# Memory-augmented attention in segments: turning the softmax rows by VectorE block transposes instead of TensorE

## The chip, the cores and the metric

The kernel runs on one core of a Trainium2 chip. A core has a matrix engine (TensorE, PE in the profile; PEld is its weight load), a vector engine (VectorE, DVE), a scalar engine (ScalarE, ACT), GpSimd (POOL) and a queue engine that issues transfers (SyncE, SP). SBUF is the working memory of 128 partitions; PSUM takes what TensorE writes. The metric is the time of one execution on the device in microseconds.

## The reference: what is computed

The input is x of 2048 rows by 512. Four layers follow each other, each added to its input after a layer normalization: attention A, dense B, attention A, dense B, with the same weights in both rounds.

```python
def _A_ref(x, mem0, Wq, Wk, Wv, Wo, seg_len):      # seg_len 32, 32 heads of 128, memory of 8 rows
    for s in range(n_seg):                         # 64 segments
        h = concatenate([mem, xs])                 # 40 rows
        q, k, v = h @ Wq, h @ Wk, h @ Wv           # per head
        scores = where(mask, q @ k.T * scale, -1e9)
        p = softmax(scores)
        o = (p @ v) @ Wo
        mem = o[:, :M, :]
        outs.append(o[:, M:, :])
def _B_ref(x, w1, w2):                             # 512 -> 1376 -> 512
    return relu(x @ w1) @ w2
x = x + A(layernorm(x)); x = x + B(layernorm(x)); x = x + A(layernorm(x)); x = x + B(layernorm(x))
```

The memory rows that a segment puts out are the memory of the next one, so the 64 segments of a round follow each other.

## The kernel before

The two rounds run together. In step k the kernel handles segment k of the first round and segment k - 2 of the second (`DELTA`), 66 steps in all, 62 of them with both. The 40 rows of both segments stand side by side as 80 columns of `HT`, so that one weight load serves both.

A step has these parts. `queries_keys` multiplies `HT` with the weights of four heads at a time (16 matmuls of 80 columns for queries, 16 for keys) and evicts the result to `qT` and `kT`. `step_values` computes the values (`values`, L1040). The 32 heads are handled in five units (`UNITS`, L18): three of eight heads, and the last eight heads in two units of four. For each unit `scores` (L1116) multiplies queries and keys into PSUM tile `sp` (L1133), adds the mask into `es` (`block`, L1144), subtracts the row maximum (`top`, `sub`), takes the exponential on ScalarE (`exp`, L1155), sums and inverts (`total`, `recip`) and multiplies into the bf16 tile `P` (`mul`, L1175, on VectorE or GpSimd). Then the rows have to be turned, since the next matmul wants keys on the partitions: `turn` (L1181) multiplies blocks of `P` of 128 columns by an identity on TensorE into another PSUM tile `tp`, and two `keep` evictions (L1194), one for each half of the partitions, copy it to `PT`, each multiplied by a column of ones and zeros (`half`) so that the other half becomes zero. `attend` (L1205) multiplies the values with `PT` (L1217) and evicts to `OT`; `project` (L1233) multiplies by `Wo` into the PSUM tile `st`, accumulating over all heads. From there the memory columns go to the `HT` of the next step (`ev`, with which that step can start), and the rows to `OX`.

`finish` (L899) handles the dense layer of a step: `OX` is turned by a transfer (`turn`, on the SP queue) into `y`, added to the residual `xg` (64 rows of 512: 32 of each round), normalized (`layernorm`, L744: `stats`, `aggr`, the power -0.5 on GpSimd in `rstd`, `norm`), turned on TensorE (`turned`, L764, four matmuls), and multiplied by `w1` and `w2` (`dense_layer`, L785). `total` adds the result in two instructions, each of 64 rows by 256. The first round's 32 rows are normalized and turned again for the second attention; `carry`, `widen` and `narrow` copy rows on GpSimd, and `store` writes the output.

The order of all instructions is made by a planner in the kernel's own text, before the program is built (`Plan`, L289). Each operation has a list of engines with a cost for each (`t_act`, `t_dve`, `t_pool`, `t_copy`), and what it reads and writes. TensorE's operations stand in an order fixed by a table of places (`PLACE`: a place within a step for each operation and phase); those of the other engines are taken by priority, worked out backwards from their users, among those that can start within `LOOK` of the earliest. Each operation that may run on either of two engines goes to the one on which it would end first. Matmuls can run as whole tiles of 128 columns of weights or as two tiles of 64 (`PAIRED` names those that take the halves); a switch between the forms is charged. The planner also charges for TensorE's instructions being fetched in blocks of 256 (`BLOCK`, `FETCH`). Transfers are issued on the SP queue in the planner's order: value loads, the turning of `OX`, stores.

Of the kernel before, what the change touches and what calls it, by code (L numbers as in the profile page):

```python
# [8 lines left out]
BF = mybir.dt.bfloat16  # L9
# [21 lines left out]
LOOK = 0.0763052  # L31
PERIOD = 26.155362
PLACE = {
# [1342 lines left out]
```

## Time and profile before

| What | Value |
|---|---|
| three timed runs | 1589.28, 1590.21, 1590.93 us (median 1590.21) |
| profiled execution: span from the first to the last instruction | 1588.6 us (no other time of it is given) |
| busy in the span: PE | 1569.5 us, 99%, 45458 matmuls |
| ACT | 1165.2 us, 73%, 3073 instructions |
| DVE | 1082.3 us, 68%, 2957 instructions |
| POOL | 314.3 us, 20%, 667 instructions |
| granted TensorE clock, mean | 0.998 |

The profiled execution is another one than the timed runs; its span stands 1.6 us below their median. Busy time is the union of an engine's instructions, which overlap by their pipelines, above all on PE; what an instruction costs in a stream without gaps is read from the distance between the starts of two. In the timeline each line has the start, the time from the first start to the last end of a group, engine, line of the kernel, operation, what it writes and reads, and the number of instructions; in brackets stands the idle time of the engine before it and what ended it. In the groups the numbers after the bar are busy time, mean duration in ns of one, and the engine's idle time before them.

### The profile page before, as it was taken

The numbers are of one execution on the slowest core, as the hardware profiler recorded it, in microseconds if no ns is written. First come the engines' busy times: TensorE is split into PE (matmuls) and PEld (weight loads), VectorE is DVE, ScalarE is ACT, GpSimd is POOL, SyncE is SP. The second block draws the span as 40 slices with busy tenths as digits, with TensorE's granted clock in tenths as the row PEclk, the third lists the DMA queues.
The fourth block names the chain that finished last, engine by engine and source line by source line (L and its number), as shares of the span: only waits on it lengthen the run. The fifth ranks groups of instructions, "written<-read, shape, count | busy, mean of one in ns | idle before, by whom it ended". The sixth has DMA issues, their size and how long they took to land.

```text
span 1588.6 us, 100346 instructions
## 1 busy us (share of the span) xinstructions
PE 1569.5 (99%) x45458; PEld 1411.1 (89%) x45458; DVE 1082.3 (68%) x2957; ACT 1165.2 (73%) x3073; POOL 314.3 (20%) x667
## 2 busy tenths in 40 slices
PE   8999999999999999999999999999999999999998
PEld 5689999999999989999989999999998998898887
DVE  4566766766776776686676677677667667667665
ACT  4667777777777777777777777777777777777774
POOL 5112112212112212121121221211211121112110
PEclk9999999999999999999999999999999999999999
DMA  9711111111111111111111111111111111111100
GB/s 371 243 44 30 26 33 32 29 35 37 25 39 31 35 29 33 29 32 40 26 36 27 35 26 42 37 26 38 25 35 28 33 33 29 33 25 22 28 21 9
DMA packets 76540, 70.89 MB, mean 45 GB/s; under 512 B 50920, under 2 KB 62416, under 8 KB 76112
## 3 DMA queue, kind: packets, MB, share of 16 engines
q1 hardware_dynamic: 70096, 44.14, 13.1%
q0 software_dynamic: 4992, 19.40, 3.4%
q8 instruction: 356, 5.83, 1.6%
q10 hardware_dynamic: 1024, 0.93, 0.2%
q14 instruction: 72, 0.59, 0.1%
HBM read 31.53 MB, written 9.96 MB: 26 GB/s over the span
## 4 chain that ended last, share of the span: by engine, by line
PE 97%; DMA 1%; DVE 1%; POOL 1%; ACT 0%; issue 0%; DVEq 0%; POOLq 0%
PE work L726 40%; PE st L726 19%; PE fill L1048 16%; PE fill L726 8%; PE fill L821 5%; PE work L1217 5%; PE work L1133 4%; DMA xg<-in_A_x_dram 0%; DMA y<-OX 0%; DMA w_sb<-in_B_w_dram 0%; ACT HT L982 0%; POOL Wo_sb L537 0%; PE fill L711 0%; DVE ln L749 0%; POOL ln L736 0%
## 5 line engine op out<-in xcount | busy, mean ns | idle before, releaser
L726 PE MATMUL work<-HT,Wq_sb 128*128 128x80 bf16 (+2 forms) x10400 | 361.8, 201 | 3.1 <-ACT HT L982 3.1
L726 PE MATMUL work<-HT,Wk_sb 128*128 128x80 bf16 (+2 forms) x10416 | 362.7, 201 | 0.8 <-ACT HT L982 0.8
L726 PEld LDWEIGHTS <-Wq_sb 128*128 128x128 bf16 (+1 forms) x10400 | 330.9, 104 | 20.8 <-issue 6.0
L726 PE MATMUL st<-OT,Wo_sb 128*128 128x80 bf16 (+1 forms) x8448 | 345.5, 201 | 0.0
L726 PEld LDWEIGHTS <-Wk_sb 128*128 128x128 bf16 (+1 forms) x10416 | 327.1, 104 | 17.3 <-issue 2.0
L726 PEld LDWEIGHTS <-Wo_sb 128*128 128x128 bf16 x8448 | 315.7, 100 | 13.0 <-issue 12.7
L1048 PE MATMUL fill<-Wv_sb,HT 128*64 128x512 bf16 x2112 | 273.6, 381 | 1.1 <-DVE HT L984 1.0
L982 ACT CAST kT<-work 128x320 bf16<-128x320 f32 (+1 forms) x523 | 218.3, 418 | 68.6 <-PE work L726 31.1
L982 ACT CAST qT<-work 128x320 bf16<-128x320 f32 (+1 forms) x516 | 215.7, 418 | 67.5 <-PE work L726 47.2
L1198 ACT ACTIVATE PT<-work,half 128x160 bf16<-128x160 f32 (+1 forms) x515 | 231.3, 463 | 20.1 <-PE work L726 12.7
L982 ACT CAST OT<-work 128x320 bf16<-128x320 f32 (+1 forms) x461 | 186.2, 420 | 50.7 <-PE work L1217 50.6
L982 ACT CAST vw<-fill 128x512 bf16<-128x512 f32 x229 | 134.1, 586 | 113.3 <-PE fill L1048 109.8
L1144 DVE TENSOR_TENSOR es<-work,maskb 128x320 f32<-128x320 f32 (+2 forms) x330 | 136.2, 413 | 99.7 <-PE work L1133 93.2
L924 DVE TENSOR_TENSOR xg<-xg,y 64x512 f32<-64x512 f32 x65 | 44.2, 680 | 227.2 <-DMA y<-OX 226.6
L731 POOL TENSOR_SCALAR ln<-ln 32x1 f32<-32x1 f32 (+2 forms) x159 | 46.6, 293 | 566.7 <-DVE ln L752 561.0
L1155 ACT ACTIVATE es<-es 128x320 f32<-128x320 f32 (+2 forms) x330 | 136.1, 413 | 24.4 <-DVE es L1151 16.2
L1048 PEld LDWEIGHTS <-HT 128*64 128x64 bf16 x2112 | 98.9, 110 | 57.0 <-DVE HT L984 1.2
L1151 DVE TENSOR_TENSOR es<-es,mx 128x320 f32<-128x320 f32 (+2 forms) x330 | 136.3, 413 | 4.9
L1148 DVE TENSOR_REDUCE mx<-es 128x8 f32<-128x320 f32 (+2 forms) x330 | 133.9, 406 | 5.4
L1158 DVE TENSOR_REDUCE sm<-es 128x8 f32<-128x320 f32 (+2 forms) x330 | 133.4, 404 | 5.1 <-ACT es L1155 2.2
L1175 DVE TENSOR_TENSOR P<-es,sm 128x320 bf16<-128x320 f32 (+1 forms) x269 | 126.9, 472 | 3.3
L1133 PEld LDWEIGHTS <-qT 128*40 128x40 bf16 x4096 | 93.3, 97 | 35.6 <-ACT qT L982 13.6
(96 smaller groups left out, 2164.8 us busy)
## 6 DMA issues: line engine op xcount, KB each, us to landing
V<-vw SPq DMA_DIRECT2D x248, 48.0 KB
V<-vh SPq DMA_DIRECT2D x120, 64.0 KB
Wq_sb<-in_A_Wq_dram POOLq DMA_DIRECT2D x2, 2048.0 KB, 23.2
Wk_sb<-in_A_Wk_dram POOLq DMA_DIRECT2D x2, 2048.0 KB, 28.6
Wo_sb<-in_A_Wo_dram POOLq DMA_DIRECT2D x2, 2048.0 KB, 39.4
vh<-vg SPq DMA_DIRECT2D x32, 128.0 KB
xb<-in_A_x_dram SPq DMA_DIRECT2D x16, 128.0 KB
Wv_sb<-in_A_Wv_dram POOLq DMA_DIRECT2D x1, 2048.0 KB, 13.2
```

What stands on the lines that cost most here:

```text
L726: nc.tensor.matmul(out_[u:v, :], lhsT=lhsT[:, u:v], rhs=rhs, start=start, stop=stop, tile_position=(0, u), **more)
L821: nc.tensor.matmul(yp[64 * u:64 * u + 64, 0:256], lhsT=hT[:, fc, :], rhs=w2_sb[:, fc, 256 * u:256 * u + 256], start=(fc == 0), stop=(fc == ...
L982: nc.scalar.copy(out=out_, in_=in_)
L1048: nc.tensor.matmul(vp[64 * b:64 * b + 64, :], lhsT=cols(c4), rhs=Wv_sb[:, c4, n * 512:(n + 1) * 512], start=(c4 == 0), stop=(c4 == NC4 - 1 ...
L1133: nc.tensor.matmul(v[64 * g2:64 * g2 + L, a, i, b, :], lhsT=qT[:, hi, a * L:(a + 1) * L], rhs=kT[:, hi, a * L:(a + 1) * L], start=True, st ...
L1144: nc.vector.tensor_tensor(out=flat(es[:, A]), in0=flat(sp[:, A]), op=ALU.add, in1=maskb[:, a_lo:a_hi, :].unsqueeze(2).to_broadcast([128, n ...
L1148: nc.vector.tensor_reduce(out=mx[:, As], in_=es3(), axis=AX.X, op=ALU.max)
L1151: nc.vector.tensor_tensor(out=es3(), in0=es3(), op=ALU.subtract, in1=mx[:, As].unsqueeze(2).to_broadcast([128, ns * na, L]))
L1155: nc.scalar.activation(out=es[:, A], in_=es[:, A], func=ACTF.Exp, scale=SCALE)
L1158: nc.vector.tensor_reduce(out=sm[:, As], in_=es3(), axis=AX.X, op=ALU.add)
L1175: (nc.gpsimd if eng == POOL else nc.vector).tensor_tensor(out=o, in0=flat(es[:, A]), op=ALU.mult, in1=sm[:, As].rearrange("p (a s) -> p a ...
L1198: nc.scalar.activation(out=o, in_=i, func=ACTF.Copy, scale=half[:, b:b + 1])
```

## The change

1. `BLOCKED = (0, 1, 2, 3)`: in all units the softmax rows are turned without TensorE. The scores of two heads are laid down next to each other, so that in `es` and `P` the two heads alternate from key to key. A pair of bf16 values then makes one 4-byte element. `mul` (VectorE only, two instructions for a unit of eight heads) writes `P`; `turn` is one `nc.vector.transpose` of 4-byte elements, which turns blocks of 32 by 32 in place and puts them into `es`. Narrow copies place the blocks in `PT`: for each half of the partitions `stay` copies the blocks that lie in the right partitions (64 partitions), `shift` the others in two instructions (32 partitions each, 8 and 32 keys for each pair of heads). They run on ScalarE or GpSimd. The rest of `PT` is zero from three fills at the start, so `half` is not used for it. `attend` reads its moving operand at every second bf16 element (`spread`), since the heads alternate. The PSUM tile `tp` is gone; `es` has three buffers instead of two.
2. The residual rows stand as 128 partitions by 256 columns instead of 64 by 512 (the second half of the columns in other partitions). So the instructions of `finish` on VectorE take half the elements: `layernorm_halves` computes statistics of half rows, exchanges them between the partition halves (`swap`, two tiny copies) and combines them. `turned` needs two matmuls instead of four, `total` one instruction instead of two; the turning transfer of `OX` has two blocks instead of four; `carry` and `widen` are two instructions each, and the store is two transfers.
3. The order is planned anew: other `PLACE`, `PAIRED` and `AHEAD` tables, and `LOOK` of 0.1008 instead of 0.0763. In the program that results, 12,000 query and key matmuls run as half-width ones instead of 7,840, TensorE has 46,090 matmuls instead of 45,458, and 289 switches of the tile form instead of 299. GpSimd makes no product of the softmax any more.

```diff
-LOOK = 0.0763052
+LOOK = 0.1007903
+BLOCKED = (0, 1, 2, 3)
+def t_place(n):
+    return 0.21 + 1.16e-3 * n
...
-    p_es = ring("es", 2, [128, 8 * L], F32)
-    p_PT = ring("PT", 3, [128, 2, 4, 2, L])
+    p_es = ring("es", 3, [128, 8 * L], F32)
+    p_PT, p_PM = ring("PT", 3, [128, 4, 2, 128]), ring("PM", 0, [128, 2, 4, 2, L])
...
+        parts += [([t], 0.6, ["PT0"]) for t in p_PT.tiles]
...
+    def layernorm_halves(x, keys, quick=False):
+        def stats():
+            nc.vector.bn_stats(out=ln[:, 0:6], in_=x[:, :])
+        def swap(eng):
+            for u in range(2):
+                copy_on(eng, ln[64 * u:64 * u + 64, 8:14], ln[64 - 64 * u:128 - 64 * u, 0:6])
+        def aggr():
+            nc.vector.bn_aggr(out=ln[:, 6:8], in_=ln[:, :].rearrange("p (s f) -> p s f", s=2)[:, :, 0:6])
+        def norm():
+            nc.vector.tensor_scalar(out=xn[:, 0:256], in0=x[:, :], scalar1=ln[:, 6:7], scalar2=ln[:, 7:8],
+                                    op0=ALU.subtract, op1=ALU.mult)
+        plan.op(DVE, t_dve(256), stats, r=keys, w=[ln])
+        plan.op((ACT, DVE), (0.2, 0.2), swap, w=[ln])
...
-    def turned(xn, n, columns, copies):
+    def turned(xn, n, columns, copies, blocks=NC4):
...
-            for c4 in range(NC4):
-                across(cols, tp[:, c4 * n:(c4 + 1) * n], xn[:, c4 * 128:(c4 + 1) * 128], columns)
+            for c4 in range(blocks):
+                across(cols, tp[:, c4 * wide:(c4 + 1) * wide], xn[:, c4 * 128:(c4 + 1) * 128], columns)
...
-            for u in range(2):
-                cs = slice(256 * u, 256 * u + 256)
-                nc.vector.tensor_tensor(out=to[RB, cs], in0=x[RB, cs], in1=yp[64 * u:64 * u + 64, 0:256], op=ALU.add)
+            nc.vector.tensor_tensor(out=to[:, :], in0=x[:, :], in1=yp[:, 0:256], op=ALU.add)
...
+            for u in range(2):
+                def store(u=u):
...
+                plan.op(SP, 0.78, store, r=[ob], lag=2.45)
...
+    def moved(eng, out_, in_):
+        if eng == ACT:
+            nc.scalar.copy(out=out_, in_=in_)
+        else:
+            nc.gpsimd.tensor_copy(out=out_, in_=in_)
...
-        plan.op(PE, nx * na * 0.0358, turn, r=[*[("P", p, b, x) for b in range(2) for x in xs], "ident"], w=[tp, PT],
-                tile=EITHER, count=nx * na)
-
+        def turn():
+            nc.vector.transpose(out=es[:, 0:64 * nj].rearrange("p (j k) -> p j k", k=64),
+                                in_=P[:, 0:512].bitcast(F32).rearrange("p (j k) -> p j k", k=64)[:, mine, :])
...
+        plan.op(DVE, 0.09 + 1.06e-3 * 64 * nj, turn, r=[*where, "PT0"], w=[es, PT])
         for b in range(2):
-            def keep(eng, b=b):
...
-            copy_op(n, keep, r=[tp, PT, "half"], w=[(PT, b)], more=MASKED)
+            def stay(eng, b=b):
+                i, o = turned_pairs()
+                R = slice(64 * b, 64 * b + 64)
+                moved(eng, o[R, :, b, 0:L], i[R, :, 0:L])
+            def shift(eng, b=b):
+                i, o = turned_pairs()
+                for c, w in ((0, L - 32), (1, 32)):
+                    R, T = slice(64 * b + 32 * c, 64 * b + 32 * c + 32), slice(64 * b + 32 - 32 * c, 64 * b + 64 - 32 * c)
+                    moved(eng, o[R, :, b, 32 - 32 * c:32 - 32 * c + w], i[T, :, 32 * c:32 * c + w])
...
+        def spread(a, i, g):
+            if p in BLOCKED:
+                return PT[:, (a - a_lo) * nx + i, :, :].rearrange("p b (q g) -> p b q g", g=2)[:, :, 0:L, g]
...
-                                             rhs=PT[:, a, 2 * i + h2, :, :], start=True, stop=True, tile_position=(0, u))
+                                             rhs=spread(a, i, h2), start=True, stop=True, tile_position=(0, u))
```

More of the change, by code (lines that the diff above doesn't have):

```diff
@@ new lines @@
+    ("*layernorm.aggr", 1): -200649.813, ("*layernorm.norm", 1): 22.495, ("*layernorm.stats", 1): 17.877,
+    ("*make_mask", 1): -30.313, ("*prepare_more.zero_w2", 1): -0.818, ("*rstd.power", 1): -162.931,
+    ("*rstd.raise_", 1): -0.19, ("*turned.keep", 1): 4.73, ("*turned.turn", 1): 79044.517,
+    ("*values.ev", 1): 63605.211, ("*zero_columns.zero", 1): -130570.662, ("attend.ev", 0): 57.345,
+    ("attend.ev", 1): -2.014, ("attend.ev", 2): -18232.828, ("attend.mm", 0): 121954.026, ("attend.mm", 1): 2.485,
@@ new lines @@
+    ("prep_x.cp", 1): -6.04, ("prepare.first_exp", 1): -2.682, ("prepare.get_memory", 1): -123728.422,
+    ("prepare.keep", 1): 2763.322, ("prepare.place", 1): 31317.055, ("prepare.turn", 1): -3.242,
+    ("prepare.zero", 1): 93635.535, ("prepare.zero_bank", 1): -0.856, ("prepare.zero_none", 1): 32782.739,
+    ("project.ev", 0): -10.294, ("project.ev", 1): -5.822, ("project.ev", 2): -0.574,
+    ("project.first", 1): -76604.132, ("project.mm", 0): -7842.728, ("project.mm", 2): 136193.946,
+    ("project.rows", 0): -0.268, ("project.rows", 1): -3.828, ("project.rows", 2): -80261.41,
@@ new lines @@
+    ("scores.turn", 0): 1.73, ("scores.turn", 1): -0.078, ("turned.keep", 0): -0.114, ("turned.keep.da", 0): 9.527,
+    ("turned.keep.da", 1): 52.509, ("turned.keep.da", 2): 200547.065, ("turned.keep.db", 0): 14.324,
+    ("turned.turn", 0): -106636.935, ("turned.turn.da", 0): -1.821, ("turned.turn.da", 1): -20239.724,
+    ("turned.turn.da", 2): 0.245, ("turned.turn.db", 0): -36.958, ("values.ev", 0): 148933.802,
+    ("values.mm", 0): -0.137, ("values.mm", 1): -1.627, ("values.mm", 2): 6.543, ("zero_columns.zero", 1): 0.082,
@@ L741, in rstd @@
         else:
-            plan.op(POOL, 0.80, power, r=["half"], w=[ln])
+            plan.op(POOL, 0.95, power, r=["half"], w=[ln])
     def layernorm(x, keys, R=slice(0, 128), quick=False):
@@ L787, in dense_layer @@
         n = 2 * SEG
-        xnT, xn = p_xm.buf(), layernorm(x, keys, slice(0, n), last)
-        turned(xn, n, ident[:, 0:n], [(NC4 * n, lambda: xnT[:, :, :], same, [], [xnT])])
+        xnT, xn = p_xm.buf(), layernorm_halves(x, keys, last)
+        turned(xn, n, ident[:, :], [(NC4 * n, lambda: xnT[:, :, :], same, [], [xnT])], 2)
         hT = p_h.buf()
@@ L902, in finish @@
         last = k == nsteps - 1
-        x, keys = xg[k % 2], [("x", k % 2, a) for a in range(2)]
+        x, keys = x_of[k % 2], [("x", k % 2, a) for a in range(2)]
         if 0 in act:
@@ new lines, in scores, with mul, turn, keep @@
+        if not blocked:
+            def mul(eng):
+                o = P[:, :].rearrange("p (a c) -> p a c", a=2)[:, a_lo:a_hi, 128 * xs[0]:128 * xs[-1] + 128]
+                o = o.rearrange("p a (s k) -> p a s k", k=64)[:, :, :, 0:L]
+                (nc.gpsimd if eng == POOL else nc.vector).tensor_tensor(
+                    out=o, in0=es[:, A].rearrange("p (a s k) -> p a s k", s=ns, k=L), op=ALU.mult,
+                    in1=sm[:, As].rearrange("p (a s) -> p a s", a=na).unsqueeze(3).to_broadcast([128, na, ns, L]))
+            plan.op((POOL, DVE), (t_pool(n), t_dve(n)), mul, r=[es, sm], w=where)
+            tp = b_work.buf()
+            def turn(cols):
+                rhs = ident[:, :].rearrange("p (g q) -> p g q", g=2)[:, :, 0:L]
+                for a in range(a_lo, a_hi):
+                    for i, x in enumerate(xs):
+                        z = nx * a + i
+                        c0 = 256 * a + 128 * x
+                        across(cols, tp[:, z * 2 * L:(z + 1) * 2 * L], P[:, c0:c0 + 128], rhs)
+            PT = p_PM.buf()
+            plan.op(PE, nj * 0.0358, turn, r=[*where, "ident"], w=[tp, PT], tile=EITHER, count=nj)
+            for b in range(2):
+                def keep(eng, b=b):
+                    o = PT[:, a_lo:a_hi, 0:2 * nx, b, :]
+                    i = tp[:, A].rearrange("p (a g q) -> p a g q", g=2 * nx, q=L)
+                    if eng == ACT:
+                        nc.scalar.activation(out=o, in_=i, func=ACTF.Copy, scale=half[:, b:b + 1])
+                    else:
+                        nc.vector.tensor_scalar_mul(out=o, in0=i, scalar1=half[:, b:b + 1])
+                copy_op(n, keep, r=[tp, PT, "half"], w=[(PT, b)], more=MASKED)
+            return PT
```

274 lines of the change are left out of this document (143 added, 131 removed), and 226 rows, old and new, of tables (PAIRED, PLACE).

## The prediction

> **What bounds the kernel now.** I read the page's busy shares and chain first, then the stages, the waits of TensorE and the timeline of a step. Views: the page, with instruction fetches among the DMA queues; the stages, whose columns are busy time and instruction count of PE, PEld, DVE, ACT and POOL, granted clock, DMA share, GB/s; and the waits of PE.
>
> ```profile
> span 1588.6 us, 100346 instructions
> ...
> PE 1569.5 (99%) x45458; PEld 1411.1 (89%) x45458; DVE 1082.3 (68%) x2957; ACT 1165.2 (73%) x3073; POOL 314.3 (20%) x667
> ...
> q8 instruction: 356, 5.83, 1.6%
> ...
> PE 97%; DMA 1%; DVE 1%; POOL 1%; ACT 0%; issue 0%; DVEq 0%; POOLq 0%
> ```
> ```profile
> 520.00:720.00 200.00, 200.00 (x5887) 183.17 (x5884) 140.21 (x378) 151.99 (x402) 41.25 (x87) 1.00 0.14 32
> 1478.27:1481.57 3.30, 3.30 (x134) 2.75 (x131) 3.27 (x10) 2.62 (x6) 0.00 (x0) 1.00 0.15 35
> ```
> ```profile
> PE work L726 <- ACT HT L982: 4.0, 14, 0.3
> ```
>
> In a steady stretch TensorE is busy for 200.00 of 200 us at full clock. Its longest wait in total is 4.0 us, at the memory columns that open a step. Every other engine has room (DVE 70%, ACT 76%, POOL 21% of the stretch). So a nanosecond taken from the TensorE stream is a nanosecond of the span, as long as no new wait appears. A busy PE is not PE at its peak, so its prices are read from start to start in the timeline:
>
> ```profile
> 781.90 0.26 PE L1133 MATMUL work<-kT,qT 128*40 128x40 bf16 x8
> ...
> 782.45 0.31 PE L726 MATMUL work<-ident,P 128*64 128x80 bf16 x8
> 782.59 0.21 PE L1217 MATMUL work<-PT,V 128*64 128x80 bf16 x2
> ...
> 783.30 1.32 PE L726 MATMUL st<-OT,Wo_sb 128*128 128x80 bf16 x32
> 784.46 0.24 PE L726 MATMUL work<-ident,P 128*128 128x80 bf16 x2
> ...
> 787.32 0.20 PE L1217 MATMUL work<-PT,V 128*128 128x80 bf16 x1
> ...
> 788.04 0.26 PE L726 MATMUL fill<-ident,xr 128*128 128x32 bf16 x4
> 788.15 0.73 PE L726 MATMUL st<-OT,Wo_sb 128*128 128x80 bf16 x16
> ```
> ```profile
> 803.58 0.52 PE L726 MATMUL fill<-xnM,w_sb 128*128 128x64 bf16 x12
> 803.93 0.74 PE L726 MATMUL work<-HT,Wq_sb 128*128 128x80 bf16 x16
> 804.60 0.28 PE L1133 MATMUL work<-kT,qT 128*40 128x40 bf16 x8
> ```
> ```profile
> 1478.27 0.74 PE L726 MATMUL work<-HT,Wq_sb 128*64 128x80 bf16 x32
> 1478.84 0.74 PE L726 MATMUL work<-HT,Wk_sb 128*64 128x80 bf16 x32
> ```
>
> A whole 80-column matmul costs (784.46 - 783.30) / 32, about 36 ns. A pair of half-width ones costs 0.14 / 4 = 35 ns in the turn and 0.57 / 16 = 36 ns in queries and keys: the same. A 64-column one costs 0.35 / 12 = 29 ns. The group ahead of 804.60 takes 0.67 for 16 x 36 = 0.575, so a switch between whole and half-width tiles costs 0.097.
>
> **The change part by part.** TensorE first: the turns that go, and the attend matmuls that stay.
>
> ```profile
> L1217 PE MATMUL work<-PT,V 128*128 128x80 bf16 x516 | 61.1, 202 | 1.1 <-DVE PT L1200 1.1
> L1217 PE MATMUL work<-PT,vw 128*128 128x80 bf16 x508 | 60.8, 202 | 0.0
> L726 PE MATMUL work<-ident,P 128*128 128x80 bf16 x756 | 59.3, 202 | 0.2 <-DVE P L1175 0.2
> L1217 PE MATMUL work<-PT,vw 128*64 128x80 bf16 x1032 | 54.1, 202 | 0.5 <-ACT vw L982 0.5
> L1217 PE MATMUL work<-PT,V 128*64 128x80 bf16 x1016 | 53.3, 202 | 0.0
> ...
> L726 PE MATMUL work<-ident,P 128*64 128x80 bf16 x536 | 22.0, 201 | 0.4 <-DVE OT L984 0.4
> ```
>
> 1. Softmax turns (`scores.turn`): 756 whole and 536 / 2 = 268 pairs, 1024 x 0.0357 = 36.5 us off the stream.
> 2. Turns of normalized rows (`turned`): after the dense layer four 32-column matmuls (0.11, from 788.04 to 788.15) become two of 64 columns (0.058), 64 times: 3.3 us off. Ahead of the dense layer four of 64 columns (0.117) become two of 128, twice the columns, so nothing to speak of.
> 3. Order: tile switches fall from 299 to 289 by the two listings of the programs, 10 x 0.097 = 1.0 off. Some 4,200 more half-width query and key matmuls stand in the new order, at the same price per pair: 0.
>
> The stream loses 36.5 + 3.3 + 1.0 = 40.8 us, or 0.64 us of a 23.4 us step. Now what could be put on it.
>
> 4. Instruction supply. The page's fetch queue brought 356 packets of 16 KB, one for every 256 of PE's instructions. Turns at 36 ns per instruction pair go, and half-width groups (64 instructions in 0.575 us) crowd together: in the new order one stretch per step holds 8 + 32 + 3 x 64 instructions in about 2.0 us, next to values at 16 in 0.87. Spaced by the prices above, the quickest tenth of the blocks of 256 falls to 2.9 to 3.06 us (34 blocks). The row of 1478.27 shows 134 + 131 instructions in 3.30 us with no idle: 256 in 3.2. So a turnaround above 3.2 us is excluded. At 3.2 the blocks would wait 9.5 us in all (the shortfall summed over them), at 2.9 nothing; I take the middle, 5. [...]
>
> 5. Query and key evictions. What a hand-over costs shows at the step's opening, where nothing covers it:
>
> ```profile
> 1468.97 0.73 PE L726 MATMUL st<-OT,Wo_sb 128*128 128x80 bf16 x16
> ...
> 1470.01 0.66 PE L726 MATMUL work<-HT,Wq_sb 128*128 128x80 bf16 x14 [0.30 <-ACT HT L982]
> ```
> ```profile
> 1469.74 0.21 ACT L982 CAST HT<-st 128x64 bf16<-128x64 f32 x1 [0.32 <-PE st L726]
> ```
>
> The stream of 16 ends at 1468.97 + 0.575 = 1469.545, ScalarE starts 0.195 later, takes 0.21, and PE goes on 0.06 after that: 0.465 us. A 320-element eviction (0.43) makes it 0.68. In the new order the shortest distance from a unit's last key group to its scores is 4 half-width turns and one group, 0.11 + 0.57 = 0.68: no margin, where it was 0.87. Covered it costs 0; if ScalarE is busy with a short instruction when it should start (0.2 late, 62 steps), 12. Nearest is the covered case; I take 2. The opening itself has as many uncovered steps in both orders: 0.
>
> 6. The softmax chain. For the last unit, on DVE and ACT:
>
> ```profile
> 785.37 0.49 DVE L1175 TENSOR_TENSOR P<-es,sm 128x160 bf16<-128x160 f32 x1
> ```
> ```profile
> 786.24 0.68 ACT L1198 ACTIVATE PT<-work,half 128x160 bf16<-128x160 f32 x2 [0.18 <-PE work L726]
> ```
>
> Scores end at 782.00, the product at 785.86, the masked evictions at 786.92, and attend starts at 787.32: 0.34 of its 5.3 us are left (0.06 goes to the hand-over). In the new chain the product is followed by a block transpose of 128 elements and six narrow copies, all on ScalarE for this unit. Durations are bounded by these rows:
>
> ```profile
> L1198 ACT ACTIVATE PT<-work,half 128x320 bf16<-128x320 f32 x251 | 133.1, 533 | 0.0
> ...
> L1198 ACT ACTIVATE PT<-work,half 128x160 bf16<-128x160 f32 x263 | 97.8, 396 | 19.7 <-PE work L726 12.3
> ...
> L1144 DVE TENSOR_TENSOR es<-work,maskb 128x160 f32<-128x160 f32 x136 | 43.7, 321 | 27.6 <-PE work L1133 21.3
> ...
> L957 POOL COPY xg<-vx 32x512 f32<-32x512 f32 x64 | 39.0, 609 | 12.0 <-DVE vx L940 8.3
> ...
> L1175 DVE TENSOR_TENSOR P<-es,sm 128x160 bf16<-128x160 f32 x75 | 34.2, 455 | 0.2
> ...
> L811 DVE TENSOR_SCALAR hT<-fill 128x256 bf16<-128x256 f32 x63 | 26.8, 425 | 0.5 <-PE fill L726 0.3
> ...
> L998 POOL COPY HT<-xnA 128x128 bf16<-128x128 bf16 x63 | 18.4, 292 | 477.2 <-PE work L726 453.4 <-PE fill L1048 23.7
> ...
> L982 ACT CAST HT<-st 128x64 bf16<-128x64 f32 x62 | 13.2, 213 | 21.2 <-PE st L726 21.2
> ...
> L982 ACT CAST kT<-work 128x160 bf16<-128x160 f32 x31 | 8.9, 291 | 3.7 <-PE work L726 2.2 <-ACT vx L982 0.3
> ```
>
> A transpose has no row. As one pass over 256 elements it takes 0.425 (0.32 for 160), as two passes twice that; I take one pass, the nearest operation being a 4-byte copy. Six copies at 0.213 end to end are 1.28, less with the overlap that back-to-back rows show (two of 0.396 in 0.68). So the new chain ends 0.32 + 1.1 + 0.2 = 1.6 us after the product, 0.5 later than the 1.06 now, and the new order gives this unit 5.7 to 6.2 us instead of 5.3: covered, by 0.2 to 0.6. Cost 0. The cover is the dense matmuls and projections that stand between; without it each 0.1 us would cost 62 x 0.1 = 6 us.
>
> 7. Off the path. By the listings ACT drops 133.1 + 97.8 = 231 us of masked evictions and gets 1317 narrow copies at 0.213 to 0.291 (280 to 383), some 130 other evictions at 0.4 and 168 tiny copies of statistics: +140 to +240 on 1165, at most 90% of the new span. GpSimd gets 645 placing copies at about 0.29, +190 on 314, and loses a product per step. DVE gets 330 transposes (at most 140 us) and 247 more product pieces (0.321 to 0.455 each, 79 to 112), and loses 145 masking evictions and half the elements of each dense-path instruction (512 wide becomes 256): about even. SP issues a second store per step and transposes half as much; the store's issue is queued ahead of the value loads, which have most of a step. At the start three zeroings of the new tiles delay the first normalization: 0 to 2 us, taken as 1.
>
> **Sum.** The profile names no time for this execution but its span, 1588.6; the timed runs lie 1.6 above it at the median (1589.28, 1590.21, 1590.93). So 1588.6 - 40.8 + 5 + 2 + 1 = 1555.8, plus 1.6: 1557.
>
> **The rivals.**
> (a) Instructions come at the slow end (step 4): 9.5 in place of 5, with a late eviction or two: 1563.
> (b) The softmax chain is late. DVE's product of 160 elements takes 455 ns where the addition of the same size takes 321; in the timeline GpSimd's copy of the carried rows runs beside the slow ones. With 645 more GpSimd copies, subtraction and product of each unit may pay 0.134 each; a two-pass transpose adds 0.3. That is 0.3 us beyond the cover per step, 62 x 0.3 = 19: 1576. Against it stands that the other three units have 7 to 10 us. [...] This needs 0.66 us per step to eat the whole gain.
> (c) Slower: the attend matmuls. Their moving operand, two adjacent 40-column blocks until now, is read at every second element (`spread`), which no row of this trace does. It costs nothing if the stream keeps its pace; at half pace 1024 whole and 1024 pairs of them pay 36 ns more, 73 us: 1557 + 73 = 1630. It decides from 20 ns each on. [...]
> (d) The change does not relieve TensorE: excluded as far as rows go, since the turns stand in a stream without idle time.
>
> **How the numbers follow.** Forecast 0.60 (1547 to 1562), (a) 0.12, (b) 0.19, (c) 0.09. Low end: steps 4 to 7 cost nothing, 1590.2 - 40.8 = 1549, and 2 less for how far run and sum may stand apart: 1547. High end: (b) with step 4 at its limit, 1576 + 5, 1581; beyond it lie (c) and the worst of (b), together under 0.2. Within 0.2% (3 us, about what can be told from no change) needs (b) or (c) at exactly the gain: 0.02. Slower: (c) 0.09 and 0.02 of (b). Faster: 0.87.
>
> **What would show it.** A steady stretch with PE still at 200 of 200 us and a step of 22.8 us in place of 23.4; no `ident,P` matmuls; attend rows still at 36 ns from start to start (72 would be (c)); fetch packets still one per 256 instructions, with gaps in PE that no engine explains if (a) holds; waits of attend or of the first projection on ACT, POOL or DVE if (b) holds, and the transpose's mean against 0.425. The prediction is wrong if attend slows, if the chain of the last unit exceeds 5.7 us, or if PE's stretch is not full.

## The result

The changed kernel takes 1679.91 us (median of four runs, 1679.63 to 1680.78); the kernel before took 1590.41 beside it (1589.28 to 1590.93). The ratio is 1.0568, with a 95% interval of 1.0553 to 1.0583. It is slower by 5.7%, where 1557 us and a range of 1547 to 1581 were predicted.

First the page of the changed kernel (line numbers are now its own: L1030 is the placing copy on ScalarE, L1032 the one on GpSimd, L1024 and L1026 the evictions on ScalarE and VectorE, L1185 scores, L1286 the block transpose, L1327 attend, L737 the shared matmul line).

```profile
span 1679.1 us, 103987 instructions
...
PE 1596.4 (95%) x46090; PEld 1399.8 (83%) x46090; DVE 1031.5 (61%) x3287; ACT 1374.8 (82%) x4173; POOL 499.9 (30%) x1403
...
q8 instruction: 361, 5.91, 1.5%
...
ACT 43%; PE 42%; DVE 9%; issue 5%; DMA 1%; POOL 1%; SPq 0%; DVEq 0%; ACTq 0%; POOLq 0%
```

The last line is the chain of work that ended last. It was 97% PE; now ScalarE holds 43% of it. The stage and the waits of PE, as read before:

```profile
520.00:720.00 200.00, 194.58 (x5750) 172.41 (x5748) 127.62 (x399) 168.22 (x504) 62.06 (x174) 1.00 0.12 28
```
```profile
PE work L1327 <- ACT PT L1030: 21.8, 59, 1.2
PE work L1185 <- ACT qT L1024: 12.6, 46, 0.9
...
PE work L1185 <- ACT kT L1024: 3.3, 4, 2.2
```

TensorE is no longer busy for 200 of 200 us but for 194.58, at the same clock, and ScalarE went from 152 to 168. A step takes 24.79 us in place of 23.50 (mean distance of the memory-column evictions over the middle steps). Attend waits for the placing copies and the scores wait for the queries' eviction. The named waits are the smaller part: a busy PE is not PE at its peak, and the time from start to start of its matmuls, beyond what the prices of the prediction give, is some 130 us more than before (the 90 us lost and the 40 us of matmuls that went). Most of the excess lies just ahead of attend, between attend and the next projection, and ahead of the scores, all of them places that need something from ScalarE.

So the timeline of ScalarE at the end of one step, in which the last two units are placed, with VectorE's product and transpose of the last unit and the attend that follows:

```profile
828.73 0.34 ACT L1221 ACTIVATE es<-es 128x160 f32<-128x160 f32 x1 [0.26 <-DVE es L1286]
828.97 2.01 ACT L1030 COPY PT<-es 64x80 f32<-64x80 f32 x8
831.01 0.40 ACT L1024 COPY ln<-ln 64x6 f32<-64x6 f32 x2
831.44 0.75 ACT L1024 CAST OT<-work 128x320 bf16<-128x320 f32 x2
832.08 1.49 ACT L1030 COPY PT<-es 64x80 f32<-64x80 f32 x6
833.59 0.80 ACT L1024 CAST OT<-work 128x320 bf16<-128x320 f32 x2
```
```profile
830.12 0.32 DVE L1279 TENSOR_TENSOR P<-es,sm 128x160 bf16<-128x160 f32 x1
...
830.48 0.31 DVE L1286 STREAM_TRANSPOSE es<-P 128x128 f32<-128x128 f32 x1
```
```profile
833.61 0.20 PE L1327 MATMUL work<-PT,V 128*128 128x80 bf16 x1 [0.35 <-ACT PT L1030]
```

Eight placing copies (six of unit 3 and two of unit 2) take 2.01 us, and the six of unit 4 take 1.49: about 0.25 us each, their whole duration, one after the other. The two evictions between them take 0.75, less than twice their duration of 0.43: they overlap. The prediction had given the six copies 1.1 us. The transpose of unit 4 ends at 830.79, but ScalarE comes to its copies only at 832.08, behind those of unit 3, the statistics (`ln`) and two evictions. Attend at 833.61 starts when the last copy is done: 3.2 us after the end of the product (830.44), where the prediction had 1.6; at the median of the steps it is 3.0.

### The profile page after: what moved, and what is told of

The parts are those of the page before. It is cut to its first block, busy times and chain, and to the rows that moved or that the text cites. A ratio compares the mean times of both kernels' runs of the same rounds, so it can differ in the third digit from the quotient of the medians.

```text
span 1679.1 us, 103987 instructions
## 1 busy us (share of the span) xinstructions
PE 1596.4 (95%) x46090; PEld 1399.8 (83%) x46090; DVE 1031.5 (61%) x3287; ACT 1374.8 (82%) x4173; POOL 499.9 (30%) x1403
## 4 chain that ended last, share of the span: by engine, by line
ACT 43%; PE 42%; DVE 9%; issue 5%; DMA 1%; POOL 1%; SPq 0%; DVEq 0%; ACTq 0%; POOLq 0%
PE work L737 22%; ACT PT L1030 18%; ACT OT L1024 8%; PE fill L1096 7%; PE st L737 5%; ACT kT L1024 4%; ACT vw L1024 4%; ACT es L1221 4%; PE work L1185 3%; PE fill L737 3%; DVE sm L1224 2%; ACT qT L1024 2%; ACT ln L1024 1%; DVE es L1199 1%; DVE es L1218 1%
## 5 line engine op out<-in xcount | busy, mean ns | idle before, releaser
L737 PE MATMUL work<-HT,Wq_sb 128*64 128x80 bf16 (+2 forms) x11456 | 366.0, 201 | 2.9 <-issue 2.2
L737 PE MATMUL work<-HT,Wk_sb 128*64 128x80 bf16 (+2 forms) x11440 | 360.8, 201 | 3.6 <-ACT HT L1024 3.2
L737 PEld LDWEIGHTS <-Wq_sb 128*64 128x64 bf16 (+1 forms) x11456 | 336.1, 106 | 30.6 <-issue 4.8
L737 PE MATMUL st<-OT,Wo_sb 128*128 128x80 bf16 (+1 forms) x8448 | 345.2, 200 | 9.1
L737 PEld LDWEIGHTS <-Wk_sb 128*64 128x64 bf16 (+1 forms) x11440 | 334.2, 106 | 22.6 <-issue 4.7
L737 PEld LDWEIGHTS <-Wo_sb 128*128 128x128 bf16 x8448 | 322.7, 99 | 29.8 <-issue 29.3
L1030 ACT COPY PT<-es 64x80 f32<-64x80 f32 (+6 forms) x1317 | 328.7, 250 | 21.7 <-DVE es L1286 1.2
L1032 POOL COPY PT<-es 64x160 f32<-64x160 f32 (+4 forms) x663 | 197.3, 298 | 446.3 <-DVE sm L1227 181.1
L1024 ACT CAST kT<-work 128x320 bf16<-128x320 f32 (+1 forms) x516 | 213.4, 414 | 56.1 <-PE work L737 23.5
L1024 ACT CAST qT<-work 128x320 bf16<-128x320 f32 (+1 forms) x525 | 219.3, 418 | 47.5 <-PE work L737 2.9
L742 POOL TENSOR_SCALAR ln<-ln 128x1 f32<-128x1 f32 x159 | 38.6, 243 | 581.8 <-DVE ln L788 481.4
L1024 ACT CAST vw<-fill 128x512 bf16<-128x512 f32 x258 | 150.8, 585 | 55.9 <-PE fill L1096 49.1
L1024 ACT CAST OT<-work 128x320 bf16<-128x320 f32 (+1 forms) x505 | 184.8, 427 | 13.0 <-PE work L1327 9.6
L1279 DVE TENSOR_TENSOR P<-es,sm 128x160 bf16<-128x160 f32 x516 | 163.8, 347 | 6.0
L1327 PE MATMUL work<-PT,V 128*64 128x80 bf16 (+1 forms) x1546 | 108.1, 199 | 28.6 <-ACT PT L1030 20.6
L1185 PEld LDWEIGHTS <-qT 128*40 128x40 bf16 x4096 | 83.2, 98 | 58.7 <-ACT qT L1024 47.5
```

The costliest lines, as they stand in the source:

```text
L737: nc.tensor.matmul(out_[u:v, :], lhsT=lhsT[:, u:v], rhs=rhs, start=start, stop=stop, tile_position=(0, u), **more)
L1024: nc.scalar.copy(out=out_, in_=in_)
L1030: nc.scalar.copy(out=out_, in_=in_)
L1032: nc.gpsimd.tensor_copy(out=out_, in_=in_)
L1185: nc.tensor.matmul(v[64 * t:64 * t + L, a, i, s, :], lhsT=qT[:, hi, a * L:(a + 1) * L], rhs=kT[:, hi, a * L:(a + 1) * L], start=True, stop ...
L1279: nc.vector.tensor_tensor(out=o[:, :, 0:L, :], in0=e_spread()[:, j, :, :], op=ALU.mult, in1=by_head(sm)[:, j, :].unsqueeze(2).to_broadcast ...
```

## The experiments

Each run is compared with the kernel before on the same chip (1588.5 to 1590.2 at the median). Three runs first took single suspects away.

**No placing copies on ScalarE.** In `moved`, ScalarE's branch is dropped.

```diff
-        if eng == ACT:
-            nc.scalar.copy(out=out_, in_=in_)
-        else:
+        if eng != ACT:
             nc.gpsimd.tensor_copy(out=out_, in_=in_)
```

> The changed kernel without the placing copies that the plan gives to ScalarE (1317 instructions); what they would have put into PT stays zero, so attend works on incomplete rows. The theory that ScalarE is the late engine (its narrow copies take 0.25 us each, one after the other, and hold up attend in every step) expects the time to fall below the kernel before, to 1545 to 1565 us, with PE at 199 to 200 of 200 us. The theory that GpSimd's copies slow VectorE's instructions expects 1640 us or more, since those stay. The theory that attend's strided read is at fault expects 1640 us or more as well.

Measured 1564.59 us (one run). The 1317 copies cost 115 us, more than all of the loss. A step takes 23.04 us, 0.46 less than before; the chain is 95% PE again.

**No placing copies on GpSimd.** The same with the other branch.

> The changed kernel without the placing copies that the plan gives to GpSimd (645 instructions); PT is incomplete. The ScalarE theory expects little: 1660 to 1680 us, since the last two units, on ScalarE alone, stay as late as they were. The GpSimd theory expects most of the loss to go: 1560 to 1600 us, and the product of 160 elements on VectorE back at 320 ns from 349.

Measured 1674.43 us (one run): GpSimd's copies, 663 in the trace, cost 5.5 us, little more than the 3 us over which runs of the kernel before spread. They run beside the rest.

**The attend matmuls read 40 adjacent elements** instead of every second one (`spread`).

```diff
-  return PT[:, (a - a_lo) * nx + i, :, :].rearrange("p b (q g) -> p b q g", g=2)[:, :, 0:L, g]
+  return PT[:, (a - a_lo) * nx + i, :, g * L:g * L + L]
```

> The changed kernel with attend's moving operand read as 40 adjacent elements instead of every second one (the wrong elements, in the same number). If the strided read costs anything, the time falls, to 1610 us at a half-pace read; the ScalarE theory, and the 36 ns from start to start in the trace, expect no change: 1675 to 1684 us.

Measured 1680.15 us (one run), against 1679.91: reading every second element costs nothing. Rival (c) is out.

**The second part alone.** The halved dense path stays; no unit is turned by VectorE (`BLOCKED = ()`), and order and due times are those of the kernel before.

> Part 2 of the change alone: residual rows as 128 by 256, in the changed kernel's code, with the softmax rows turned on TensorE and the tables of the kernel before. TensorE's stream loses 3.3 us of turns: with no new wait 1586 to 1588 us. If the second part brings the waits (exchange of statistics on ScalarE, two stores), it stands above 1600 us.

Measured 1598.46 us (1597.86 to 1599.56), ratio 1.0050 (1.0033 to 1.0066). This part by itself makes the kernel 8 us slower, where step 2 of the prediction counted a gain of 3.3. A step takes 23.63 us instead of 23.50. TensorE stays full by the busy time (200.00 of 200 us), so the loss has to be read from start to start. The new two-matmul turn saves nothing: 0.047 us pass behind it at the median in which nothing starts, which takes back what the two missing matmuls saved. The 8 us themselves lie at one place in each step, between a projection and the turn of the last unit's rows (lines of this run: L1243 is the product, L1026 the two copies of `swap`):

```profile
789.36 0.16 DVE L1227 RECIPROCAL sm<-sm 128x4 f32<-128x4 f32 x1
789.55 0.50 DVE L1026 COPY ln<-ln 64x6 f32<-64x6 f32 x2
790.08 0.41 DVE L1243 TENSOR_TENSOR P<-es,sm 128x160 bf16<-128x160 f32 x1
```
```profile
789.28 1.31 PE L737 MATMUL st<-OT,Wo_sb 128*128 128x80 bf16 x32
790.54 0.25 PE L737 MATMUL work<-ident,P 128*128 128x80 bf16 x2
```

The 32 matmuls of the projection need 32 x 0.036 = 1.15 us, so the turn could start at 790.43, but its product ends only at 790.49. In 62 places the turn comes late like this, by 8.0 us in all; in the kernel before it comes 0.036 us behind the projection each time. In 61 of the steps the two `swap` copies, which the kernel before does not have, stand just ahead of that product on VectorE and take 0.5 us. That they are the cause is read from the trace; no run moved them, and an order made for this part was not tried.

**What a copy costs when its neighbour starts elsewhere.** A kernel of its own, with series of 16 copies.

> A small kernel that leaves the whole computation out (its output is zeros). ScalarE, VectorE and GpSimd each run, one engine after the other, series of 16 independent f32 copies of 64 to 82 columns; a series differs from the next only in the partitions: all 128; 0 to 63; 64 to 127; 0 to 63 and 64 to 127 by turns; 32 to 63 moved to 0 to 31; 32-partition moves both ways by turns; 32-partition copies in place by turns; full width from PSUM; full width and half by turns; full width and a quarter by turns. Theory (a copy on part of the partitions does not overlap its neighbour on ScalarE): the time from start to start is 0.12 us for the full-width series and 0.20 us or more for every narrow one, and where wide and narrow alternate both pay. Rival 1 (only a change of the first partition stops the overlap): 0 to 63 alone and 64 to 127 alone keep the 0.12 us, the alternating series pay. Rival 2 (only the semaphore waits and the work around the copies made them slow in the kernel): all series show the same start to start.

The timeline of its ScalarE, mostly one row per series (start, time of the whole series, and the shape, partitions x columns of one copy; the tile's name tells the series: `low` and `high` are the halves, `swing` both by turns, `up` the second quarter moved to the first, `updown` moves both ways by turns):

```profile
2.03 2.44 ACT L36 COPY a_all<-src 128x64 f32<-128x64 f32 x16
4.37 2.46 ACT L36 COPY a_low<-src 64x66 f32<-64x66 f32 x16
6.83 2.46 ACT L36 COPY a_high<-src 64x68 f32<-64x68 f32 x16
9.30 4.15 ACT L36 COPY a_swing<-src 64x70 f32<-64x70 f32 x16
13.46 2.54 ACT L36 COPY a_up<-src 32x72 f32<-32x72 f32 x16
15.91 4.21 ACT L36 COPY a_updown<-src 32x74 f32<-32x74 f32 x16
...
28.44 0.23 ACT L36 COPY a_allpshigh<-ps 128x80 f32<-128x80 f32 x1
28.67 0.26 ACT L36 COPY a_allpshigh<-src 64x80 f32<-64x80 f32 x1
28.94 0.23 ACT L36 COPY a_allpshigh<-ps 128x80 f32<-128x80 f32 x1
...
30.46 2.67 ACT L36 COPY a_allquart<-src 128x82 f32<-128x82 f32 x16
```

Copies on all partitions, on the lower half, on the upper half, or moved from the second quarter to the first, each among its like, follow each other at about 0.15 us (9.30 - 6.83 = 2.47 for 16), though one takes 0.24. Where halves or quarters alternate it is 0.26. A full-width copy and one on the first quarter by turns, both starting at partition 0, overlap (2.67 / 16 = 0.167, the row holds both); full width (from PSUM) and the upper half by turns do not (28.94 - 28.44 = 0.50 for a pair). So my theory of narrow copies fell, and rival 1 of this run holds: it is the change of the first partition that stops the overlap, about 0.1 us each time. VectorE and GpSimd do the same:

```profile
2.17 2.71 DVE L43 COPY v_all<-src 128x64 f32<-128x64 f32 x16
...
10.60 4.47 DVE L43 COPY v_swing<-src 64x70 f32<-64x70 f32 x16
```
```profile
4.60 2.91 POOL L49 COPY g_low<-src 64x66 f32<-64x66 f32 x16
...
10.58 4.44 POOL L49 COPY g_swing<-src 64x70 f32<-64x70 f32 x16
```

The series of VectorE and GpSimd ran at the same times, so the sizes on these two may depend on each other. But in the changed kernel too GpSimd's copies that change the partition start 0.04 us behind the end of the one before, also where VectorE is idle.

From start to start VectorE's copies take 0.17 us (2.71 / 16) while the partitions stay the same and 0.28 (4.47 / 16) by turns, GpSimd's 0.18 (2.91 / 16) and 0.28 (4.44 / 16). In ScalarE's first series a copy is 0.241 us long at the mean, with (4.37 - 2.03) / 16 = 0.146 from start to start; that overlap of 0.095 us is what is lost where the first partition changes.

**All of ScalarE's placing copies on all 128 partitions**, in place: as many instructions, the same columns, no change of partition.

```diff
 def stay(eng, b=b):
     R = slice(64 * b, 64 * b + 64)
+    R = slice(0, 128) if eng == ACT else R
 ...
     R, T = ...                       # in shift
+    R, T = (slice(0, 128),) * 2 if eng == ACT else (R, T)
```

> The changed kernel with every placing copy of ScalarE made over all 128 partitions in place, the same columns and as many instructions (it writes values into the places that should stay zero, so the heads mix: that part of the computation is not the reference's). GpSimd's copies stay as they are. Theory, as the small kernel left it (neighbours on ScalarE overlap when they work on the same partitions, and a change of the partitions costs each of the two about 0.1 us: 0.150 us from start to start against 0.25): with about 21 copies a step freed of some 0.1 us each, ScalarE gets back some 2 us a step; the time falls by 80 to 115 us, to 1565 to 1600. Rival (the number of instructions and their waits cost, whatever the partitions): 1660 us or more.

Measured 1570.39 us (1568.56 to 1570.82), ratio 0.9876 (0.9860 to 0.9893). The loss is gone, with every copy still there.

```profile
PE 1541.6 (98%) x46090; PEld 1384.7 (88%) x46090; DVE 1028.4 (66%) x3287; ACT 1264.1 (81%) x4173; POOL 516.0 (33%) x1403
...
PE 95%; DVE 2%; ACT 1%; issue 1%; POOL 1%; DMA 1%; SPq 0%; DVEq 0%; POOLq 0%; ACTq 0%
```
```profile
520.00:720.00 200.00, 199.99 (x6061) 182.57 (x6059) 133.96 (x424) 166.56 (x547) 69.80 (x189) 1.00 0.13 30
```
```profile
730.76 0.34 ACT L1221 ACTIVATE es<-es 128x160 f32<-128x160 f32 x1
731.00 1.22 ACT L1030 COPY PT<-es 128x80 f32<-128x80 f32 x8
732.25 0.40 ACT L1024 COPY ln<-ln 64x6 f32<-64x6 f32 x2
732.67 0.75 ACT L1024 CAST OT<-work 128x320 bf16<-128x320 f32 x2
733.32 0.93 ACT L1030 COPY PT<-es 128x80 f32<-128x80 f32 x6
```

The same eight copies take 1.22 us instead of 2.01, the six 0.93 instead of 1.49, though one copy is as long as ever:

```profile
L1030 ACT COPY PT<-es 128x80 f32<-128x80 f32 x268 | 55.9, 259 | 1.7 <-DVE es L1286 1.6 <-ACT es L1221 0.2
```
```profile
L1030 ACT COPY PT<-es 64x80 f32<-64x80 f32 x268 | 67.8, 253 | 4.7 <-DVE es L1286 1.2
```

(The first row is this run's, the second the changed kernel's; the mean of one is the second number behind the bar.) Over the whole run ScalarE's busy time falls by 1374.8 - 1264.1 = 111 us and the time by 109.5. ScalarE's share of the span is the same, 81% against 82%, so the share does not tell whether TensorE waits for it.

**Which copies matter.** The changed kernel without ScalarE's placing copies of units 3 and 4 only.

```diff
-    moved(eng, o[R, :, b, 0:L], i[R, :, 0:L])
+    if eng == POOL or p < 3:         # and the same in shift
+        moved(eng, o[R, :, b, 0:L], i[R, :, 0:L])
```

> The changed kernel without those placing copies of units 3 and 4 that the plan gave to ScalarE; units 0 to 2 keep theirs (the output is not the reference's for these heads). These are some 800 of the 1317 copies and 0.185 of their 0.329 ms. Theory (the chain of the last units of a step carries the loss): all or nearly all of what leaving out every ScalarE copy gave comes back: 1565 to 1585 us. Rival (it is ScalarE's load as a whole that costs, wherever the copies lie): the gain goes by the share, 0.185/0.329 of 115 us, so about 1615 us.

Measured 1614.28 us (one run): 65 of the 115 us are the last units', and the other 50 go with the copies of units 0 to 2, which the prediction had priced at nothing. The expectation of the rival, by share, came out: a copy on ScalarE costs about as much wherever it lies. With attend's wait gone (2.0 us), the scores still wait for the queries:

```profile
PE work L1185 <- ACT qT L1024: 12.5, 45, 0.9
...
PE work L1329 <- ACT PT L1030: 2.0, 3, 1.2
```

**Units 3 and 4 back on TensorE**, with their masked evictions (`BLOCKED = (0, 1, 2)`, a ring of two buffers for them, and places in TensorE's order where their product is planned to end).

> Units 0 to 2 keep the VectorE block transpose and the placing copies; units 3 and 4 are turned on TensorE again, with two masked evictions each as in the kernel before, at the places in TensorE's order where their multiplication is planned to be done. The rest of the order is the changed kernel's. 12 narrow copies a step leave the end of the step; about 0.25 us of TensorE time a step comes back. Theory (the narrow copies of the last units make the loss): 1575 to 1620 us, 60 us or more below the changed kernel, with few waits of the attention matmuls left. Rival (the loss is in the order as replanned, or in the VectorE transposes): 1660 us or more. Whether it comes below 1590 is open.

Measured 1647.32 us (1646.30 to 1648.71), ratio 1.0369 (1.0352 to 1.0386): a miss, between the theory and the rival. Attend hardly waits any more, but ScalarE still makes 233 of the staying copies of units 0 to 2 (189 before this edit) and 120 pairs of the moved ones, and the scores now wait 29.4 us for the queries.

**The placing copies of units 0 to 2 on GpSimd alone**, on top of that.

```diff
-plan.op((ACT, POOL), (0.02 + t_act(L * nj), t_place(L * nj)), stay, ...)
+plan.op(POOL, t_place(L * nj), stay, ...)      # and shift likewise
```

> As the run with units 3 and 4 on TensorE, but the placing copies of units 0 to 2 all go to GpSimd (30 per cent busy in the changed kernel), none to ScalarE. Theory (a narrow copy on ScalarE delays the evictions behind it wherever it lies, those of queries and keys too): the waits for qT go from 29 us to under 10, and the time falls from 1647 to 1575 to 1605 us, near the kernel before or under it. Rival (the rest of the loss is in the order or in the VectorE transposes): 1630 us or more.

Measured 1596.68 us (1595.16 to 1598.92), ratio 1.0046 (1.0031 to 1.0061): 51 us less. No wait for queries is left among the first ones:

```profile
PE work L1338 <- POOL PT L1315: 6.5, 5, 2.9
PE fill L749 <- DVE xr L803: 5.4, 3, 4.0
PE work L749 <- ACT HT L1036: 3.9, 13, 0.4
```

So ScalarE's 531 placing copies, eight or nine a step and nearly all of units 0 to 2, were worth 51 us, although by the prediction's count these units have more time than the last one.

**VectorE may place as well**, at a higher price for ScalarE in the planner: 0.25 us and 0.85 ns per element, 0.32 us for a copy of 80 columns. (In the changed kernel these follow each other at 0.28.)

> The changed kernel with its order of TensorE kept, but the planner may put the placing copies on VectorE as well, and a copy on ScalarE costs it 0.25 us and 0.85 ns per element instead of 0.07 us and 0.83 ns: 702 copies stay on ScalarE, 674 go to VectorE (32 per cent idle in the changed kernel's stages) and 509 to GpSimd. Theory (ScalarE's copies at the end of the step make the loss): 1620 to 1660 us, part of the loss back, as VectorE lies on the same softmax chain. Rival (it does not matter where the copies lie, since every engine takes as long over them): 1675 us or more. It does not tell how many copies VectorE would take in an order made for it.

Measured 1718.61 us (1715.93 to 1719.22), ratio 1.0812 (1.0796 to 1.0828): 39 us worse, on the rival's side and beyond it. The chain is now 51% PE and 33% DVE:

```profile
PE work L1333 <- DVE PT L1036: 65.0, 40, 3.3
PE work L1333 <- ACT PT L1034: 23.3, 13, 3.3
PE st L741 <- DVE OT L1030: 19.7, 33, 0.6
```

Attend waits 65 us for VectorE's placing copies and the projection 20 us for evictions of `OT` that moved there. VectorE had 39% idle time in the changed kernel, but the softmax of the next unit and these copies are on the same engine.

**Keeping ScalarE at full width with the whole computation.** The copy that stays in its partitions is made over all of them, scaled by the 0/1 column; the moved ones go to GpSimd, or to ScalarE at that higher price.

```diff
+if eng == ACT:
+    nc.scalar.activation(out=o[:, :, b, 0:L], in_=i[:, :, 0:L], func=ACTF.Copy, scale=half[:, b:b + 1])
```

> The whole computation again: the changed kernel, with each copy that stays in its partitions done by ScalarE over all 128 of them, scaled by the 0/1 column that the masked evictions of the kernel before use (the other half receives the zeros it needs); the copies that move by 32 partitions go to GpSimd, or to ScalarE at the price measured, 0.25 us and 0.85 ns per element. TensorE's order is the changed kernel's. Theory (only a change of the partitions costs ScalarE its overlap): between the run with all copies at full width (1570) and the changed kernel (1680), nearer the first since about half of the moved copies leave ScalarE too: 1580 to 1605. Rival (the masked form costs as much as a narrow copy): 1640 or more.

Measured 1622.29 us (1620.32 to 1624.45), ratio 1.0209 (1.0194 to 1.0224): 58 us better than the changed kernel, but not in the range. The masked form is longer by about 0.1 us:

```profile
L1302 ACT ACTIVATE PT<-es,half 128x80 f32<-128x80 f32 x267 | 81.2, 351 | 5.7 <-DVE es L1290 4.2
```

0.351 against 0.259 for the plain full-width copy. From start to start it takes 0.26 at the median of back-to-back pairs, where the plain full-width copy takes 0.16 and the narrow one 0.28. So neighbours still overlap (267 x 0.351 = 93.7 us, in 81.2 busy), but the scale column adds as much as the overlap saves: 0.351 - 0.259 = 0.092 us for 80 columns. For 160 columns the masked copy takes 0.434 in this run, and the exponential of `es`, without a column, 0.336.

The same operations in an order searched anew:

> The same operations as the run before it, with TensorE's order and the planner's due times searched anew with these prices. Theory: the gain that the change was worth on TensorE (36.5 + 3.3 us less) shows once ScalarE keeps its overlap: 1568 to 1585 us, faster than the kernel before; 1570 is what the run with all copies at full width took. Rival (the moved copies, still narrow and now later in the chain, cost what the turn on TensorE cost): 1588 or more.

Measured 1611.27 us (1610.73 to 1612.32), ratio 1.0142 (1.0125 to 1.0159): 11 us from the order, and still slower than before. The search had the masked copy 0.1 us too cheap.

**The best whole kernel found.** Units 3 and 4 on TensorE, units 0 to 2 placed by GpSimd, order and due times searched anew.

> The same operations as the run with units 3 and 4 on TensorE and all placing copies of units 0 to 2 on GpSimd (1597), with TensorE's order and the planner's due times searched anew for them. Theory (what is left against the sums is the order alone: with three units' turns gone, 756 matmuls of 36 ns or 27 us, a run that loses nothing would take about 1563, and 1597 loses 34 in waits spread over all groups): part of the 34 comes back, 1575 to 1588 us, under the kernel before. Rival (the part that the halved dense path costs, 8 us alone, and GpSimd's longer chain stay whatever the order): 1590 us or more.

Measured 1588.50 us (1586.19 to 1591.37, eleven runs) against 1589.61, ratio 0.9996 (0.9987 to 1.0005). It is level with the kernel before, no faster: 8 us came back by the order. It lies in neither range. Part of what keeps it from its sum is at the start: the first eviction of memory columns comes at 111.4 us of the span instead of 107.0, while the 61 distances from there to the last one are 6.5 us shorter in all than in the kernel before. The rest is not settled; its longest waits, up to 4.3 us in total, are mostly those that the kernel before had, and VectorE's share of the chain is 21%.

## Why the prediction was wrong

**Steps 1 and 3, the stream of TensorE: mostly right.** Where nothing on ScalarE holds it (the run without its copies), a step takes 23.04 us, 0.46 less than before, and the time is 1564.6. Of the 40.8 us counted, less the 8 that steps 4, 5 and 7 were to cost, 25.6 came in place of 32.8. Two things make up most of the difference: the two-matmul turn saves nothing (3.3 us, step 2), and the first eviction of memory columns comes at 111.3 us of the span instead of 107.0, 4.3 us later where step 7 counted 1.

**Step 2, the halved dense path: wrong sign.** +8.3 us alone in place of -3.3. The two wide turning matmuls save nothing with what follows them, and the exchange of statistics, which the prediction counted as a load of ScalarE alone, makes the last unit's product late for its turn on TensorE: 8.0 us. The changed kernel has no such turn, so this second loss cannot come back there.

**Step 4, instruction supply, and rival (a): no sign of it.** 361 packets, as forecast one per 256 instructions. In the run with full-width copies, which has the same half-width crowds at full pace, the distances between half-width query and key matmuls hold six gaps over 80 ns, 1.4 us in all. No run shows the 5 us that the sum took for this step; these 1.4 us are what was found in their place.

**Step 5, query and key evictions: right with a free ScalarE, wrong with a busy one.** 2 was taken, 12 was the other end. Without ScalarE's copies PE waits 2.2 us there for queries and keys, in the changed kernel 12.6 + 3.3. The case that was to cost 12 ("if ScalarE is busy with a short instruction when it should start") is the case that came.

**Step 6, the softmax chain of the last unit: the step that failed first.** The transpose was right: one pass, 0.434 us for 256 elements and 0.282 for 128, taken as 0.425 and 0.32. The copies' durations were nearly right: means of 0.194 to 0.323, taken as 0.213 to 0.291. What was wrong is "less with the overlap that back-to-back rows show (two of 0.396 in 0.68)". That overlap belongs to evictions that start at the same partition (in the small kernel 0.15 us from start to start, against 0.26 where the start changes). Five of the six placing copies start elsewhere than the one before them, and the eviction behind them once more: 1.49 us instead of 1.1. The larger part is that unit 3's copies, slowed in the same way, stand ahead of them on the same queue, which the sum left out: attend starts 3.0 us after the product in place of 1.6, the cover of 0.2 to 0.6 is gone, and the last units' copies cost 65 us in place of 0.

**Step 7, off the path: the number right, its price wrong.** ScalarE was to gain 140 to 240 us and gained 1374.8 - 1165.2 = 210. "At most 90%" was read as harmless. But the evictions of queries, keys and attention output stand in the same queue, and they are what TensorE waits for next: 50 us come from units 0 to 2, whose own chain has 7 to 10 us by the prediction's count. A queue with 18% idle time over a step has stretches without any: in the step shown ScalarE works from 828.73 to 834.39 without a pause.

**The rivals.** (b), a late softmax chain, had the right place and a chance of 0.19, but its causes were others (VectorE slowed by GpSimd's copies, a transpose of two passes) and it stopped at 19 us. The slowing is there and small: the subtraction of 160 elements takes 0.376 us (0.32 in the kernel before, and 0.321 again without GpSimd's copies), and leaving out all of these copies gains 5.5 us. (c) cost nothing: 1680.15 us with adjacent elements against 1679.91 with every second one. No rival let ScalarE's queue become the bound.

## What to carry to other kernels

Price an instruction by the time from start to start among the neighbours that it will have, not by its duration: on these three engines a copy that starts at another partition than the one before it pays about 0.1 us, and so does the next one that goes back (in the small kernel 0.26 us from start to start against 0.15 on ScalarE, 0.28 against 0.17 on VectorE and 0.18 on GpSimd). When work moves to an engine that has room on average, list what stands behind it in that engine's queue and which engine waits for that; the slack of the moved work's own chain says nothing about it. Here turning the softmax rows without TensorE cost time as long as ScalarE, which empties PSUM, did the placing; with three units placed by GpSimd and two units back on TensorE it came out level, and no whole kernel that was tried beat the kernel before.

## What the runs showed of the hardware that was not expected

Back-to-back copies of 64 to 76 columns within SBUF follow each other at 0.15 us on ScalarE, and at 0.16 to 0.18 on VectorE and GpSimd, which ran beside each other, while the first partition stays the same, on 128, 64 and 32 partitions alike; when it changes they follow at 0.26 to 0.28. The duration of one copy in the profile, 0.23 to 0.27 us, is nearly the same in both cases, so no row of means shows it. Narrowness by itself cost nothing in the small kernel: 16 copies on ScalarE take 2.44 us on 128 partitions (64 columns), 2.46 on 64 (66 columns) and 2.54 on 32 (72 columns). A per-partition scale on ScalarE adds 0.09 us to a copy of 80 columns (0.351 against 0.259), and about 0.1 from start to start (0.26 against 0.16).
